# Mamba-2 scan with a silu MLP on one core: masked B^T x in PSUM, another order of weight pieces, loads and sums

## The chip, the cores and the metric

The kernel runs on one core of one Trainium2 chip. The metric is device microseconds of one execution. The engines are TensorE (PE in the profile, its weight loads PEld), VectorE (DVE), ScalarE (ACT), GpSimd (POOL) and SyncE (SP, which here only issues DMAs). Each takes its own instructions in the order in which the program lists them; between engines, semaphores hold an instruction until its inputs and buffers are ready.

## What is computed

A scan over 4 batches of 8 heads, 768 steps, head size 32 and state size 16, and an MLP on its result, 3072 tokens wide 256, with 2048 hidden units. The reference uses chunks of 32 steps; the result doesn't depend on the length of a chunk, and the kernel uses 64.

```
for c in range(nc):                      # chunks, in order
    cum = cumsum(log a)                  # within the chunk
    M = (C B^T) * exp(cum_i - cum_j) * causal
    y = M x + (C state) * exp(cum_i)
    state = exp(sum log a) * state + sum_j exp(cum_last - cum_j) B_j x_j
h = y @ w_in;  g = h / (1 + exp(-h));  out = g @ w_out
```

## The kernel before

**Units.** The work is cut into 12 units of 256 steps, three to a batch (u = 0 to 11; u % 3 == 2 is the last of its batch and needs no state after it). Each unit holds four chunks of 64 steps, t = 0 to 3, written as t = 2k + c.

**The scan of a unit** runs through these functions:
- `load_unit` issues the unit's DMAs on SP's queue: `pa` and `ab` (a in two layouts), B and C (`bn`, `tbc`), and `xt` (x). Units 1 and 2 take C in the layout of `bn`, and TensorE transposes both (`f_TP`, L333); later ones use VectorE (`f_T`, L324).
- `f_P` (L262, L268) makes prefix products of a, `f_E` (L299, L281) the decays E.
- `f_B` (L318) on POOL: BT = B times the decay to the end of the chunk. `f_C` (L349): C times the prefix.
- `f_G` is `f_D0` (L367), B^T x of each chunk by matmuls, then `f_G0` (L382), C B^T. From unit 2 on both land in one PSUM tile, `gy`, [128, 4, 512], which fills four banks and has a single buffer: C B^T in columns 0 to 255 of each bank, B^T x in columns 256 to 383 of banks 0 and 1 (the bank is c). Columns 384 to 511 are unused.
- `f_M` (L393) on VectorE multiplies C B^T into E.
- `f_D` (L402) on ScalarE: two heads share each group of 32 rows, so B^T x has blocks that mix heads. Each of four instructions copies a part with a mask (`par`) as its scale to the SBUF tile `dm`.
- `f_S` makes the states one after the other: state(t+1) = state(t) * decay + dm(t), for each chunk. The first of a batch is a copy (L416), the others one VectorE instruction (L424), except from unit 4 on for the last update of a unit, which is two POOL instructions (L421, L422).
- `f_Y` takes a new `gy` tile, in the same buffer, and writes y to it: first C times state (L444), then M x (L453). `f_X` (L462) copies it to SBUF as XM on ScalarE.

**The MLP.** `f_s1` (L473, silu L475) does h and g of a unit for 256 hidden units, j = 0 to 7; `f_s2` runs the next few matmuls of the output (L487, L564) from a list of generators. From unit 4 on, units are taken in pairs, and a 2 x 2 block product with seven products in place of eight is used: `f_x1` (L647 to L661) for h, `s2_pair` for the output. It needs sums of the operands: `f_SW` (of w_in, POOL, L619), `f_SO` (of w_out, VectorE, L518), `f_XT` (of x, POOL, L630) and `f_TS` (of g, POOL, L532). `sums(P, j)` calls `f_TS` for the parts of pair P that are due at step j.

**Weights.** They come as 8-byte floats in 16 pieces of 512 KB (0 to 7 of w_in, 8 to 15 of w_out). `w_size(n)` (ScalarE, L164, L166) and `w_bits(n)` (VectorE L174, L176, L178, then POOL L182) make float32 of piece n. There are seven raw buffers, and `w_bits(n)` ends with the DMA of piece n + 7, in SP's queue. `wu` and `wv` between the two have three buffers.

**The order** is written out by hand: what stands earlier in the program stands earlier in each engine's queue. The list `steps` interleaves `f_s1` of units 0 and 1 with weight pieces ("s5" is `w_size(5)`, "b5" `w_bits(5)`) and with unit 2's scan (letters of `scan_piece`: T transposes, E decays, B is `f_B` and `f_C`, G is `f_G`, `f_M`, `f_D` and `f_S`, Y is `f_Y` and `f_X`, S one `f_SW`). `late` does so in unit 2's loop. From there on loops run over j = 0 to 7 for unit 2 (scan of unit 3 between), for unit 3 (scans of 4 and 5 between) and for the pairs G = 2 to 5 (scan of the next pair between, `scan_plan`).

Of the kernel before, what the change touches and what calls it, by code (L numbers as in the profile page):

```python
# [8 lines left out]
FP32 = mybir.dt.float32  # L9
# [3 lines left out]
ALU = mybir.AluOpType  # L13
# [8 lines left out]
def kernel(  # L22
# [101 lines left out]
    def load_unit(u):  # L124
        load_pa(u, nc.sync)
        if 0 < u < UPB:
            load_n(u, 1, nc.sync)
        else:
            load_t(u, 0, nc.sync)
            load_t(u, 1, nc.sync)  # L130
        load_ab(u, nc.sync)
        load_n(u, 0, nc.sync)
        load_x(u, nc.sync)
# [26 lines left out]
    def w_size(n):  # L160
        if n in raw:
            u = wu[n] = wtp.tile([128, 2, WF], FP32, name="wu")
            v = wv[n] = wtp.tile([128, 2, WF], FP32, name="wv")
            nc.scalar.activation(u, raw[n][:, :, :, 1].bitcast(FP32), AF.Abs)  # L164

            nc.scalar.activation(v, raw[n][:, :, :, 0], AF.Copy, scale=2.0 ** -51, bias=2.0)  # L166

    def w_bits(n, parts=1):
        dst = w_piece(n)[1]
        if n in raw:  # L170
            u, v, hi = wu.pop(n), wv.pop(n).bitcast(U32), raw[n][:, :, :, 1]


            nc.vector.tensor_scalar(out=u, in0=u, scalar1=LEAST, scalar2=MOST, op0=ALU.max, op1=ALU.min)  # L174
            u = u.bitcast(U32)
            nc.vector.tensor_scalar(out=u, in0=u, scalar1=3, scalar2=None, op0=ALU.logical_shift_left)  # L176

            nc.vector.scalar_tensor_tensor(out=v, in0=hi, scalar=0x80000000, in1=v,  # L178
                                           op0=ALU.bitwise_and, op1=ALU.bitwise_or)
            for i in range(parts):  # L180
                fs = slice(WF // parts * i, WF // parts * (i + 1))
                nc.gpsimd.tensor_tensor(out=dst[:, :, fs].bitcast(U32), in0=u[:, :, fs], in1=v[:, :, fs], op=ALU.add)  # L182
        if n + RAW < len(W):
            load_w(n + RAW, nc.sync)
# [16 lines left out]
    load_x(1, nc.sync)  # L201
    for n in range(3, RAW):
        load_w(n, nc.sync)
    load_unit(2)


    def f_A():
# [144 lines left out]
    def f_D0(u, early=False):  # L352

        last = u % UPB == UPB - 1
        bt = BT.pop(u).rearrange("p k h n -> p k (h n)")
        xc = xt[u].rearrange("p k h d -> p k (h d)")
        n = 3 if last else 4
        if early:
            d = [ps_h.tile([128, 512], FP32, name="hp")[:, 0:128] for c in range(2)]
        else:  # L360
            DP[u] = ps_s.tile([128, 4, 512], FP32, name="gy")
            d = [DP[u][:, c, 256:384] for c in range(2)]
        d = [o.rearrange("p (k x) -> p k x", k=2) for o in d]
        for t in range(n):
            k, c = divmod(t, 2)
            for g in range(4):
                nc.tensor.matmul(out=d[c][32 * g:32 * g + 32, k],  # L367
                                 lhsT=bt[64 * c:64 * c + 64, k, 32 * g:32 * g + 32],
                                 rhs=xc[64 * c:64 * c + 64, k, 64 * g:64 * g + 64], start=True, stop=True,
                                 tile_position=(64 * c, 32 * g), skip_group_check=True)  # L370
        BX[u] = d, n

    def f_G0(u):

# [19 lines left out]

    def f_D(u, c):

        d, n = BX[u]
        if c == 0:
            DM[u] = sc.tile([128, 2, 2, 64], FP32, name="dm")
        nk = (n + 1 - c) // 2  # L400
        for e in range(2):
            nc.scalar.activation(DM[u][:, 0:nk, c, 32 * e:32 * e + 32], d[c][:, 0:nk, 32 * e:32 * e + 32],  # L402
                                 AF.Copy, scale=par[:, e:e + 1])

    def f_S(u, t0=0, t1=4):

        first, last = u % UPB == 0, u % UPB == UPB - 1
        if first and t0 == 0:
            ST[u] = sc2.tile([128, 4, 64], FP32, name="st")
        if not last and t1 == 4:  # L410
            ST[u + 1] = sc2.tile([128, 4, 64], FP32, name="st")
        for t in range(t0, min(t1, 3 if last else 4)):
            k, c = divmod(t, 2)
            o = ST[u][:, t + 1] if t < 3 else ST[u + 1][:, 0]
            if first and t == 0:
                nc.vector.tensor_copy(out=o, in_=DM[u][:, k, c])  # L416
            else:
                p = PFX[u][:, t, Q:]
                if u >= 2 * UPB - 2 and t == (2 if last else 3):

                    nc.gpsimd.tensor_tensor(out=o, in0=ST[u][:, t], in1=p.to_broadcast([128, 64]), op=ALU.mult)  # L421
                    nc.gpsimd.tensor_tensor(out=o, in0=o, in1=DM[u][:, k, c], op=ALU.add)  # L422
                else:
                    nc.vector.scalar_tensor_tensor(out=o, in0=ST[u][:, t], scalar=p,  # L424
                                                   in1=DM[u][:, k, c], op0=ALU.mult, op1=ALU.add)

    def f_GMD(u):
        f_G(u)
# [30 lines left out]
    def f_X(u):  # L459

        XM[u] = xmp.tile([128, 4, 128], FP32, name="XM")
        nc.scalar.activation(XM[u], DP.pop(u)[:, :, 0:128], AF.Copy)  # L462


    def f_s1(g, j):
        if j == 0:
            GTS[g] = gpool.tile([128, NF, UT], FP32, name="gT")
        xm = XM[g].rearrange("p (w c) t -> p w (c t)", w=2)
        hp = ps_h.tile([128, 2, UT], FP32, name="hp")
        for i in range(2):  # L470
            f = 2 * j + i
            for kc in range(KC):
                nc.tensor.matmul(out=hp[:, i], lhsT=w_in_sb[:, kc, f * 128:(f + 1) * 128],  # L473
                                 rhs=xm[:, kc], start=(kc == 0), stop=(kc == KC - 1))
        nc.scalar.activation(GTS[g][:, 2 * j:2 * j + 2], hp, AF.Silu)  # L475
        if j == 7:
            XM.pop(g)
# [295 lines left out]
    f_Ab(1, 0)  # L773
    f_Ab(1, 1)
    w_size(1)
    w_size(2)
    busy(2)
    f_Y(0)
    f_X(0)
    w_bits(1)  # L780
    f_s1(0, 0)
    f_Ek(1, 0)
    f_TP(1, True)
# [16 lines left out]
    for k in range(2):  # L800
        f_M(1, k)
    w_size(4)
    f_S(1)
    f_s1(0, 3)
    f_Y(1)
    f_X(1)
    w_bits(4)

    steps = ((1, 0, "s5"), (1, 1, "b5 s6"), (1, 2, "b6 s7"), (1, 3, "E"), (0, 4, "b7 s8"),
             (1, 4, "T B"), (0, 5, "b8 s9"), (1, 5, "G"), (0, 6, "b9 s10"), (1, 6, "b10 s11"),  # L810
             (0, 7, "Y"), (1, 7, "b11 s12"))

    def w_steps(todo):
        for step in todo.split():
# [6 lines left out]
        f_s1(g, j)  # L821
        w_steps(todo)
    load_unit(3)
    late = ("b12 s13", "b13 s14", "b14 s15 b15")
    S2.append(s2_list((0, 1)))
    for j in range(8):
        f_s1(2, j)
        scan_piece(3, j, ("", "", "T", "E", "BS", "G", "", "Y"))
        f_s2(4)
        if j < len(late):  # L830
            w_steps(late[j])
        if j in (2, 5):
            load_unit(4 + j // 3)
    def sums(P, j):

        for q in {4: (0, 1), 5: (2,), 8: (3,)}.get(j, ()):
            f_TS(P, 0, q, nc.gpsimd)
            f_TS(P, 2, q, nc.gpsimd)

    for j in range(8):  # L840
        f_s1(3, j)
        scan_piece(4, j, ("TE", "BS", "G", "Y", "", "", "", ""))
        scan_piece(5, j, ("", "", "T", "E", "BSS", "G", "Y", ""))
        scan_piece(6, j, ("",) * 7 + ("t",))
        f_s2(4)
        if j in (2, 5):
            load_unit(6 + j // 3)
        if j >= 6:
            f_SO(2 * j - 12)
            f_SO(2 * j - 11)  # L850
        if j == 7:
            for i in range(4):
                f_XT(2, i)
        if j == 5:
            sums(1, 4)
    for G in range(2, NU // 2):
        S2.append(s2_pair(G - 1))
        more = G + 1 < NU // 2
        plan = scan_plan(G + 1) if more else [([], [], []) for _ in range(8)]
        for j, (dve, act, pe) in enumerate(plan):  # L860
            waiting, PEND[:] = PEND[:], []
            f_x1(G, j, dve, act)
            for what in pe:
                what()
            for what in waiting:
                what()
            if j == 1:
                if G == 2:
                    sums(1, 5)
                sums(G - 1, 8)  # L870
            if j == 1 or j == 2:
                for q in range(4):
                    f_TS(G - 1, 2 * j - 1, q, nc.gpsimd)
            if j == 6 and more:
                for i in range(4):
                    f_XT(G + 1, i)
            sums(G, j)
            if j in (2, 5) and 2 * G + 4 + j // 3 < NU:
                load_unit(2 * G + 4 + j // 3)
    P = NU // 2 - 1  # L880
    sums(P, 8)
    S2.append(s2_pair(P, True))
    for n in range(7):
        f_s2(8)
# [37 lines left out]
```

## Time and profile before

| What | us |
|---|---|
| Median of 4 runs | 367.93 (366.99, 367.21, 368.64, 375.56) |
| Profiled execution, whole | 366.68 |
| Its span, first to last instruction | 364.8 |
| Groups (sum): L473 / L564 / L647 matmuls 128x256 | 59.6 / 56.5 / 52.8 and more |
| L424, state update on VectorE, x32 | 0.275 / 0.285 / 0.770 (least, median, most of one) |
| L421 + L422 on POOL, x8 each | 0.292 and 0.320 (medians) |
| L402, masked copy to `dm`, x40 of `gy` | 0.313 (median) |
| L532, a sum of g on POOL | 0.78 (mean) |
| L619, a sum of w_in on POOL | 2.35 |

How to read it: busy time is a sum over instructions of an engine; one of TensorE overlaps the next, so steps between starts tell its pace. A line of waits names the waiting engine and line, what ended the wait, and then the sum in us, the number of times and the longest. A timeline row has start, duration, engine, line, operation, output<-inputs, shapes and a count; in brackets stand the idle time before it and what ended it. The DMA queue issues in order, and its rows are SP's time for the issue, not the transfer. The first 29 us are start-up, in which the engines wait for loads and for one another; from there TensorE's matmuls follow one another almost without a break until 356 us.

### The profile page before, as it was taken

How to read it: one execution, taken by the hardware profiler on the slowest of the kernel's cores; microseconds unless marked ns; L12 is line 12 of the kernel's file. 1: busy time of each engine (PE TensorE's matmuls, PEld its weight loads, DVE VectorE, ACT ScalarE, POOL GpSimd, SP SyncE). 2: the span in 40 equal slices, each digit the busy share in tenths (PEclk: the TensorE clock that was granted, in tenths of full speed). 3: DMA queues.
4: the chain of work that ended last, by engine and by line, in shares of the span. 5: the costliest groups of instructions: out<-in, count | busy, mean ns of one | idle time of the engine just before them, and what ended most of it. 6: DMA issues, size and time to landing. Idle time of an engine off the chain costs nothing.

```text
span 364.8 us, 8354 instructions
## 1 busy us (share of the span) xinstructions
PE 347.7 (95%) x3277; PEld 289.5 (79%) x3279; DVE 190.4 (52%) x383; ACT 162.7 (45%) x414; POOL 188.8 (52%) x259
## 2 busy tenths in 40 slices
PE   8689899999999899999999999999999999999994
PEld 2467688788887688878887878888878888888883
DVE  7985988652348647743445742456742221213722
ACT  2565755423232444545444644544644444554100
POOL 3432344233057759896159496149595646473100
PEclk9999999999999999999999999999999999999998
DMA  6998956861545242152127034110000110001202
GB/s 141 195 273 174 353 153 113 134 114 42 109 106 72 66 78 32 17 117 38 22 52 111 14 100 52 26 16 2 14 2 6 25 16 1 14 2 17 41 2 44
DMA packets 110195, 26.53 MB, mean 73 GB/s; under 512 B 98892, under 2 KB 106060, under 8 KB 110156
## 3 DMA queue, kind: packets, MB, share of 16 engines
q1 hardware_dynamic: 107180, 25.67, 34.2%
q10 hardware_dynamic: 2976, 0.33, 0.6%
q8 instruction: 26, 0.43, 0.5%
q14 instruction: 13, 0.11, 0.1%
HBM read 22.83 MB, written 3.15 MB: 71 GB/s over the span
## 4 chain that ended last, share of the span: by engine, by line
PE 68%; POOL 9%; DVE 6%; issue 5%; DMA 5%; ACT 3%; SPq 3%; ACTq 0%; DVEq 0%; POOLq 0%
PE o_ps L564 27%; PE hp L647 24%; PE hp L473 5%; PE o_ps L487 4%; PE hp L564 3%; POOL gT L532 3%; PE gy L453 2%; POOL TN L532 2%; DMA raw<-in_moe_w_in_dram 2%; DVE wv L178 1%; PE gy L382 1%; POOL raw L619 1%; DMA xt<-in_x_dram 1%; PE gy L444 1%; ACT wu L164 1%
## 5 line engine op out<-in xcount | busy, mean ns | idle before, releaser
L650 DVE TENSOR_TENSOR gT<-hp,p 128x256 f32<-128x256 f32 x64 | 26.9, 420 | 83.1 <-ACT p L661 45.0
L473 PE MATMUL hp<-XM,w_in_sb 128*128 128x256 f32 x256 | 59.6, 381 | 4.5 <-ACT XM L462 3.3
L653 ACT ACTIVATE gT<-gT 128x256 f32<-128x256 f32 x96 | 39.8, 414 | 44.3 <-DVE gT L650 44.3
L473 PEld LDWEIGHTS hp<-XM,w_in_sb 128*128 128x128 f32 x256 | 48.0, 190 | 11.9 <-POOL w_in_sb L182 4.6
L564 PE MATMUL o_ps<-gT,w_out_sb 128*128 128x256 f32 x224 | 56.5, 379 | 0.0
L647 PE MATMUL hp<-raw 128*128 128x256 f32 x192 | 52.8, 380 | 1.5 <-POOL raw L630 1.5
L532 POOL TENSOR_TENSOR gT<-gT 128x256 f32<-128x256 f32 x72 | 54.2, 780 | 0.0
L564 PEld LDWEIGHTS o_ps<-gT,w_out_sb 128*128 128x128 f32 x224 | 42.5, 190 | 5.9
L647 PEld LDWEIGHTS hp<-raw 128*128 128x128 f32 x192 | 36.0, 190 | 7.3 <-POOL raw L630 1.9
L535 POOL TENSOR_TENSOR ps<-ps 128x256 f32<-128x256 f32 x28 | 20.3, 725 | 41.1 <-ACT ps L571 34.5
L318 POOL TENSOR_TENSOR BT<-bn,E 128x256 f32<-128x256 f32 x12 | 7.9, 654 | 60.9 <-DMA out_dram<-ot 18.4
L661 ACT ACTIVATE p<-hp 128x256 f32<-128x256 f32 x64 | 24.5, 383 | 30.2 <-PE hp L647 28.5
L475 ACT ACTIVATE gT<-hp 128x512 f32<-128x512 f32 x32 | 19.0, 598 | 39.6 <-PE hp L473 39.6
L647 PE MATMUL hp<-XM,w_in_sb 128*128 128x256 f32 x128 | 34.2, 389 | 0.0
L650 DVE TENSOR_TENSOR gT<-hp,u 128x256 f32<-128x256 f32 x32 | 13.5, 422 | 35.7 <-PE hp L647 35.7
L487 PE MATMUL o_ps<-w_out_sb,gT 128*128 128x256 f32 x128 | 31.1, 385 | 0.6 <-POOL w_out_sb L182 0.6
L532 POOL TENSOR_TENSOR TN<-gT 128x256 f32<-128x256 f32 x40 | 30.1, 772 | 0.1
L487 PEld LDWEIGHTS o_ps<-w_out_sb,gT 128*128 128x128 f32 x128 | 23.7, 190 | 4.7 <-POOL w_out_sb L182 1.0
L647 PEld LDWEIGHTS hp<-XM,w_in_sb 128*128 128x128 f32 x128 | 23.2, 189 | 4.4 <-issue 1.0
L281 DVE TENSOR_TENSOR_SCAN E<-ab,diag 128x256 f32<-128x256 f32 (+1 forms) x32 | 24.9, 819 | 2.7 <-PE gy L453 2.3
L393 DVE TENSOR_TENSOR E<-gy,E 128x512 f32<-128x512 f32 x24 | 15.4, 681 | 19.5 <-PE gy L382 15.7
L532 POOL TENSOR_TENSOR gT<-gT,TN 128x256 f32<-128x256 f32 x32 | 22.1, 728 | 0.0
(123 smaller groups left out, 556.0 us busy)
## 6 DMA issues: line engine op xcount, KB each, us to landing
ab<-in_a_dram SPq DMA_DIRECT2D x40, 128.0 KB, 3.7
raw<-in_moe_w_in_dram SPq DMA_DIRECT2D x8, 512.0 KB, 4.4
raw<-in_moe_w_out_dram SPq DMA_DIRECT2D x8, 512.0 KB, 3.6
xt<-in_x_dram SPq DMA_DIRECT2D x24, 128.0 KB, 3.4
out_dram<-ot SPq DMA_DIRECT2D x76, 32.0 KB, 1.7
pa<-in_a_dram SPq DMA_DIRECT2D x12, 128.0 KB
bn<-in_B_dram SPq DMA_DIRECT2D x22, 64.0 KB, 3.9
tbc<-in_C_dram SPq DMA_DIRECT2D x40, 32.0 KB, 1.9
```

What stands on the lines that cost most here:

```text
L281: nc.vector.tensor_tensor_scan(out=E[u].rearrange("p k h t -> p (k h t)")[:, Q * g0:Q * (g0 + n)], data0=t.rearrange("p g t -> p (g t)"), ...
L393: nc.vector.tensor_tensor(out=m[:, k], in0=DP[u][:, :, 128 * k:128 * k + 128], in1=m[:, k], op=ALU.mult)
L473: nc.tensor.matmul(out=hp[:, i], lhsT=w_in_sb[:, kc, f * 128:(f + 1) * 128], rhs=xm[:, kc], start=(kc == 0), stop=(kc == KC - 1))
L475: nc.scalar.activation(GTS[g][:, 2 * j:2 * j + 2], hp, AF.Silu)
L487: nc.tensor.matmul(out=o[:, c], lhsT=GTS[g][:, f, 128 * c:128 * c + 128], rhs=w_out_sb[:, f, :], start=(f == 0), stop=(f == NF - 1), skip_ ...
L532: engine.tensor_tensor(out=o[:, j], in0=a0[:, j], in1=a1[:, j], op=ALU.subtract)
L535: engine.tensor_tensor(out=o, in0=p, in1=q, op=ALU.add)
L564: nc.tensor.matmul(out=o, lhsT=w(j), rhs=g()[:, j], start=(j == 0), stop=(j == NF // 2 - 1))
L647: nc.tensor.matmul(out=o, lhsT=w, rhs=x_, start=start, stop=True, skip_group_check=True)
L650: nc.vector.tensor_tensor(out=o, in0=p, in1=q, op=ALU.add)
L653: nc.scalar.activation(o, i, AF.Silu)
L661: nc.scalar.activation(o, i, AF.Copy)
```

## The change

Three parts. First, for units 2 and on, ScalarE's masked copy of B^T x goes to columns 384 to 511 of the same `gy` tile, where there is room, and not to SBUF. All state updates are on VectorE and read it there; POOL's two instructions are gone. Units 0 and 1 (`early`) keep a `dm` tile in SBUF. Second, the order of the beginning: `load_unit(2)` stands behind the loads of pieces 7 and 8, `w_size(2)` behind unit 0's `f_X`, the preparation of pieces 5 to 8 stands earlier, and unit 2's E, T, B, G and Y earlier in `steps`. The last pieces get other places in `late`, and the second, third and fourth `f_SW` stand one call earlier (one of them now in unit 2's loop). Third, of the sums of g of the first pair only the first part stays in unit 3's loop, ahead of `f_XT(2, i)`; the second follows behind the first step of pair 2, and the others in its second step.

```diff
-    load_unit(2)
...
+        dm = None if early else [DP[u][:, c, 384:512].rearrange("p (k x) -> p k x", k=2) for c in range(2)]
...
-        BX[u] = d, n
+        BX[u] = d, dm, n
...
-        d, n = BX[u]
+        d, dm, n = BX[u]
         if c == 0:
-            DM[u] = sc.tile([128, 2, 2, 64], FP32, name="dm")
+            if dm is None:
+                dm = sc.tile([128, 2, 2, 64], FP32, name="dm")
+                dm = [dm[:, 0], dm[:, 1]]
+            DM[u] = dm
         nk = (n + 1 - c) // 2
         for e in range(2):
-            nc.scalar.activation(DM[u][:, 0:nk, c, 32 * e:32 * e + 32], d[c][:, 0:nk, 32 * e:32 * e + 32],
+            nc.scalar.activation(DM[u][c][:, 0:nk, 32 * e:32 * e + 32], d[c][:, 0:nk, 32 * e:32 * e + 32],
                                  AF.Copy, scale=par[:, e:e + 1])
...
             if first and t == 0:
-                nc.vector.tensor_copy(out=o, in_=DM[u][:, k, c])
+                nc.vector.tensor_copy(out=o, in_=DM[u][c][:, k])
             else:
-                p = PFX[u][:, t, Q:]
-                if u >= 2 * UPB - 2 and t == (2 if last else 3):
-
-                    nc.gpsimd.tensor_tensor(out=o, in0=ST[u][:, t], in1=p.to_broadcast([128, 64]), op=ALU.mult)
-                    nc.gpsimd.tensor_tensor(out=o, in0=o, in1=DM[u][:, k, c], op=ALU.add)
-                else:
-                    nc.vector.scalar_tensor_tensor(out=o, in0=ST[u][:, t], scalar=p,
-                                                   in1=DM[u][:, k, c], op0=ALU.mult, op1=ALU.add)
+                nc.vector.scalar_tensor_tensor(out=o, in0=ST[u][:, t], scalar=PFX[u][:, t, Q:],
+                                               in1=DM[u][c][:, k], op0=ALU.mult, op1=ALU.add)
...
     w_size(1)
-    w_size(2)
     busy(2)
     f_Y(0)
     f_X(0)
+    w_size(2)
     w_bits(1)
+    load_unit(2)
...
     w_size(4)
+    w_size(5)
     f_S(1)
     f_s1(0, 3)
     f_Y(1)
     f_X(1)
+    w_size(6)
     w_bits(4)
+    w_bits(5)
-    steps = ((1, 0, "s5"), (1, 1, "b5 s6"), (1, 2, "b6 s7"), (1, 3, "E"), (0, 4, "b7 s8"),
-             (1, 4, "T B"), (0, 5, "b8 s9"), (1, 5, "G"), (0, 6, "b9 s10"), (1, 6, "b10 s11"),
-             (0, 7, "Y"), (1, 7, "b11 s12"))
+    steps = ((1, 0, "b6 s7"), (1, 1, "E"), (1, 2, "T B b7 s8"), (1, 3, "b8 s9"), (0, 4, ""),
+             (1, 4, "G b9 s10"), (0, 5, ""), (1, 5, "Y b10 s11"), (0, 6, "b11 s12"), (1, 6, ""),
+             (0, 7, "b12 s13"), (1, 7, ""))
...
-    late = ("b12 s13", "b13 s14", "b14 s15 b15")
+    late = ("b13 s14", "b14 s15", "b15")
...
-        scan_piece(3, j, ("", "", "T", "E", "BS", "G", "", "Y"))
+        scan_piece(3, j, ("", "", "T", "E", "BS", "G", "S", "Y"))
...
-    def sums(P, j):
-
-        for q in {4: (0, 1), 5: (2,), 8: (3,)}.get(j, ()):
+    def sums(P, qs):
+
+        for q in qs:
...
-        scan_piece(5, j, ("", "", "T", "E", "BSS", "G", "Y", ""))
+        scan_piece(5, j, ("", "", "T", "E", "BS", "G", "Y", ""))
...
         if j == 5:
-            sums(1, 4)
+            sums(1, (0,))
...
+            if G == 2 and j == 0:
+                sums(1, (1,))
             if j == 1:
-                if G == 2:
-                    sums(1, 5)
-                sums(G - 1, 8)
+                sums(G - 1, (2, 3) if G == 2 else (3,))
...
-            sums(G, j)
+            sums(G, {4: (0, 1), 5: (2,)}.get(j, ()))
...
-    sums(P, 8)
+    sums(P, (3,))
```

## The prediction, made before the changed kernel had run

> **What bounds the kernel now.** First the page's table of busy times and the granted clock, to see which engine is the limit:
>
> ```profile
> PE 347.7 (95%) x3277; PEld 289.5 (79%) x3279; DVE 190.4 (52%) x383; ACT 162.7 (45%) x414; POOL 188.8 (52%) x259
> PEclk9999999999999999999999999999999999999998
> ```
>
> TensorE is busy 95% at full clock; the others have half their time free. So a change that leaves the matmuls alone can only win what TensorE stands idle, and only work that makes TensorE wait can lose. The second view is therefore the list of waits of TensorE alone (us in total, times, longest):
>
> ```profile
> PE hp L473 <- ACT XM L462: 3.3, 2, 2.5
> PE gy L444 <- POOL st L422: 1.8, 3, 0.8
> PE gy L367 <- POOL BT L318: 1.6, 1, 1.6
> PE hp L647 <- POOL raw L630: 1.5, 1, 1.5
> PE hp L473 <- POOL w_in_sb L182: 1.2, 2, 0.9
> PE o_ps L487 <- POOL w_out_sb L182: 0.6, 1, 0.6
> ```
>
> The first and fifth lie before 29.33 us (start-up); the rest lie later. Over 29.3 to 356 us the windows view gives 321.0 busy of 326.7, so at most about 6 us, and a little that modelled ends hide, is to be had there. The third view is the timeline, for where these waits stand and what stood in the queue ahead:
>
> ```profile
> 45.41 0.43 PE L367 MATMUL gy<-xt,BT 64*32 64x64 f32 x24 [1.56 <-POOL BT L318]
> ...
> 112.72 0.58 PE L444 MATMUL gy<-cw,st 32*64 32x64 f32 x24
> 113.89 0.34 PE L444 MATMUL gy<-cw,st 32*64 32x64 f32 x8 [0.59 <-POOL st L422]
> ...
> 122.74 0.70 PE L647 MATMUL hp<-raw 128*128 128x256 f32 x2 [1.48 <-POOL raw L630]
> ```
>
> The step from one start to the next is safer than a modelled end. Where nothing waits a 256-column matmul starts every 216 ns; against that the stops are 1.73 us (from 43.47), 0.75 (67.74, weight piece 15) and 1.64 (120.88, the differences of X). For the state updates I read from the first L444 to the first L453: 0.63 where nothing waits (unit 4, 32 matmuls), 0.51 with 24. Unit 5 takes 1.44, unit 6 0.72, unit 7 1.03, unit 8 1.63, unit 9 1.04, unit 10 0.63, unit 11 1.48: an excess of 0.81, 0.21, 0.40, 1.00, 0.53, 0 and 0.85, 3.8 in all. POOL's two-instruction update is behind sums in its queue there, and VectorE's own ones are slow:
>
> ```profile
> 98.12 1.01 DVE L424 SCALAR_TENSOR_TENSOR st<-st,pfx,dm 128x64 f32<-128x64 f32 x3 [0.67 <-ACT dm L402]
> ...
> 140.50 1.29 DVE L424 SCALAR_TENSOR_TENSOR st<-st,pfx,dm 128x64 f32<-128x64 f32 x2
> ```
>
> At 98 us POOL is idle and three take 1.01; at 140 us POOL runs sums and two take 1.29.
>
> **What the skill says.** "SBUF — State Buffer", Who interferes with whom: a VectorE instruction with two SBUF inputs and a GpSimd one that reads SBUF block each other wholly, while one with at most one SBUF input, outside the two-port modes, does not contend. The trace agrees: L424 runs from 0.28 to 0.77, while L650, with one PSUM input, stays at 0.42 in the middle of POOL's sums. "PSUM — Partial Sum Buffer", PSUM bank collisions: two engines must be kept from the same bank at once, reads against reads too. The trace has it as a wait: dm L402 waits on E L393 (9.4 us, 4 times), which it doesn't read. "VectorE: DVE Perf Modes", The TRN2 errata: a PSUM source costs 120 cycles fixed against 58, an estimate of 65 ns more per update; no run here shows it yet.
>
> **The change part by part.**
>
> *States from PSUM, all on VectorE (units 2 to 11).* Removed: 8 times two POOL instructions (0.29 + 0.32, 0.67 + 0.65 once). Added: 8 VectorE updates. Cost of one: between 0.22 (copy-like, below SBUF) and 0.35 (0.285 + 0.065); I take 0.29, step 0.34, because L650 with a PSUM input costs no more than its size suggests. ScalarE's write goes to PSUM instead of SBUF: 0.31 now, between 0.25 and 0.37; I take no change, as its step of 0.2 isn't what ends the wait except in odd units. Added wait: the y tile of L444 takes the same buffer as gy, so all of y waits until the last update has read dm, also the one (t = 3) that only the next unit needs. Behind that wait stands the whole TensorE queue. So, unit by unit, from the first update now:
> - Unit 5: updates end at about 112.65, y wanted at 112.72. Excess 0.81 to 0.05: 0.76.
> - Unit 6: first at 139.69, copy unblocked 0.2, three at 0.34: 140.95 against 141.40: 0.21.
> - Unit 7: ScalarE's dm ends at 161.87; the last update ends 162.85 against 162.66, so y starts 0.2 late: gain 0.2.
> - Unit 8: three from 194.41 end 195.4 against 196.12: 1.00.
> - Unit 9: end at 218.28 against 218.06: 0.53 to 0.25: 0.28.
> - Unit 10: end 251.2 against 251.56: 0. Unit 11: end 272.3 against 272.48: 0.85.
> Sum 3.3. At the dear end (0.07 more per step, up to four steps) units 5, 7 and 9 lose 0.25 each: 2.5. At the cheap end 3.7.
>
> *Sums of x before sums of g.* Before unit 3's stage ends POOL has 4 fewer sums (of 0.7 to 1.15, "113.80" to "121.97" in its timeline) ahead of the four differences at L630, and no state update. X of unit 5 is ready at 115.65, so the first difference is done by about 116.5, and TensorE wants it at 120.9. Gain 1.64. The moved four sums fall into POOL's idle 6.25 us before BT at 131.53, and the next ones stand where they stood, so nothing reads them later. The weight sums `f_SW` (2.35 each, at 73.85, 88.26 and twice from 105.92) come one call earlier: the second runs right behind the first, in an idle stretch of 10.8, and the third takes its place at 88.26. There it can hold back VectorE's prefix and clamp of unit 4, but the scan behind them waits until 84.47 anyway: 0. The 8 added updates, 2.4 us of VectorE, lie in its idle half.
>
> *Pieces 5 to 8, unit 2's scan sooner.* `w_size(2)` behind XM(0): XM starts near 13.4 instead of 15.20, the first stage 1.4 earlier. It doesn't last: the third (21.23) waits for piece 2, which is VectorE, without a break from 12.01 to 21.7, and POOL. 0. ScalarE's `w_size(5)` and `w_size(6)` (1.3 each) fall into its idle 1.31 and 2.08 before the silus at 27.12 and 31.36; were those gone, each would cost a silu at most 0.6, and three hp buffers cover that. The B-ahead-of-b7 order takes the 1.73 at 43.47 away: POOL's L182 of piece 7 (1.27) and VectorE's three for it stood ahead of BT. The last load of weights is issued earlier too, as b8 is, and unit 3's loads behind it. Piece 15 is prepared one step sooner (its ACT part ended at 66.4 for a read at 67.74; now some 3 us early): 0.75.
>
> Against that, unit 2's loads (11 issues, in SP's one queue) now stand behind pieces 7 and 8, each 512 KB. At the page's best slice, 353 GB/s, each takes 1.5 us: 3.0 later. SP's queue is full there (four ab issues take 7.28):
>
> ```profile
> 21.38 7.28 SPq L95 DMA_DIRECT2D ab<-in_a_dram  x4
> 28.71 2.23 SPq L107 DMA_DIRECT2D bn<-in_B_dram  x2
> 30.99 1.30 SPq L122 DMA_DIRECT2D xt<-in_x_dram  x2
> 32.41 0.73 SPq L156 DMA_DIRECT2D raw<-in_moe_w_in_dram  x1
> ```
>
> bn(2)'s second issue is at 29.4; with the page's 3.9 us to landing it is there at 33.3 now, at 36.4 after. The transposes of bn(2) on TensorE (L333) move from behind (1,4) at 39.6 to behind (1,2): 29.33 + 3 x 1.73 = 34.5. TensorE takes its queue in order, so all of it waits: about 2.0, between 0.8 (loads catch up) and 3.2 (landing as slow as C's 7.5 median suggests). After that nothing is late: E(2) ends near 38.3 (ab at 34.4, pieces 5 and 6 ahead of it), BT near 39, D at 42.4; state updates end near 46.5, Y(2) is wanted at 47.
>
> Sum: 3.3 + 1.64 + 1.73 + 0.75 - 2.0 = 5.4. The profiled execution took 366.68 (span 364.8 and 1.9 around it), so 361.3. The median of the runs shown is 367.93, 1.25 above it; without the one at 375.56 the middle is 367.21, 0.5 above. I add 0.6: 361.9.
>
> **The rivals.**
> - *The transposes' wait eats more, or the last update holds y more than I think* (dear ends together: 3.2, 2.5): 2.5 + 1.64 + 1.73 + 0.75 - 3.2 = 3.4, 363.9. For it: SP's queue is at its limit there. Against: packets flow without a gap, so 3.0 is firm.
> - *The loads are there in time* and the PSUM reads are cheap: 3.7 + 1.64 + 2.48 = 7.8, 359.5. For it: the listed bn landing is a median over the kernel.
> - *The updates don't decide* and y waits the same: banks keep ScalarE's second pair and VectorE's first apart until both are done, the chain M, D, S then being serial. 3.3 shrinks to 1: 364.2.
> - *Slower.* Unit 2's loads land so late that the transposes' wait carries on into D(2) and Y(2), since all queues are in order. Price: as many us as the landing of x is over 42.4, on top of the 2.0. It turns the sum negative when together they pass 7.4, x at 48 or so, 11 us over now. Then about 368.5 or more. Against it: x lands near 34.3 in the trace's packets, and 37.4 with two pieces ahead.
>
> **How the numbers follow.** The forecast 0.55, dear ends 0.17, in time 0.1, serial updates 0.1, slower 0.05, something unseen 0.03. The range 359.5 to 364.8 holds the first, and most of the next three. About 0.5% (1.8 us) can be told from no change: below 366.1 is faster. The first four cases lie there but for their far tails (0.03 of 0.92): 0.89; these tails and the unseen are the same, 0.06; slower 0.05.
>
> **What would show it.** Right: no L421/L422 group, L424 near 0.29 during POOL's sums, no wait of L444 over 0.3 after 100 us, none of L647 on raw, a wait of TensorE at L333 of about 2 us for bn's DMA near 34.5, BT(2) near 39. Wrong: L424 above 0.4, y held by DVE in each unit, no wait at L333, or a new one at L367.

## The result: slower, and the profile after

The changed kernel takes 370.84 us (median of 32 runs, 368.54 to 372.57) against 368.48 for the kernel before beside it (51 runs, 366.36 to 375.56). The ratio is 1.0077, 95% interval 1.006 to 1.0094; ratios leave out executions over 1.5% above the fastest of their kernel, so they aren't the quotients of the medians. The profiled execution took 369.51 us (span 367.8; before 366.68 and 364.8).

TensorE's work is the same, and it waits for others. From the page of after, busy us, share of the span and instructions of each engine:

```profile
PE 347.2 (94%) x3277; PEld 289.4 (79%) x3279; DVE 195.3 (53%) x391; ACT 165.2 (45%) x414; POOL 180.3 (49%) x243
```

TensorE's waits in after (us in total, times, longest):

```profile
PE hp L644 <- DVE gT L647: 4.2, 4, 3.0
PE gy L441 <- DVE st L421: 4.1, 6, 1.1
```

The waits for BT, for `raw` and for `w_out_sb` that stood here before are gone, and so is POOL as the one who holds the state up. Two new ones are larger than each of them. (Line numbers after: L441 is y's first matmul, L421 the state update, L405 the masked copy, L261 the clamp `pz` of `f_P`, L267 its scan, L529 a sum of g, L644 and L647 the MLP's matmul and the addition of its result.)

**The first loss: y waits for the updates.** Unit 4's masked copies and updates, which POOL does not disturb, in the timeline (start us, duration, engine, line). Before:

```profile
97.57 0.93 ACT L402 ACTIVATE dm<-gy,par 128x64 f32<-128x64 f32 x4 [1.95 <-DVE E L393]
...
98.12 1.01 DVE L424 SCALAR_TENSOR_TENSOR st<-st,pfx,dm 128x64 f32<-128x64 f32 x3 [0.67 <-ACT dm L402]
```

After:

```profile
97.31 1.25 ACT L405 ACTIVATE gy<-gy,par 128x64 f32<-128x64 f32 x4 [1.96 <-DVE E L393]
...
98.59 1.23 DVE L421 SCALAR_TENSOR_TENSOR st<-st,pfx,gy 128x64 f32<-128x64 f32 x4 [1.40 <-ACT gy L405]
```

Read the distance from the first copy to the first update: 0.55 us before, 1.28 after. Before, the four copies start 0.20 apart and overlap, and the first update starts after the second copy. After, each copy waits on ScalarE's own semaphore for the one ahead of it (0.32 from start to start), since all four now read and write one tile, and the first update waits for the fourth, though it reads only what the first two wrote. Then four updates follow rather than three. The updates themselves are as cheap as I had hoped: 0.281 us each (mean, none over 0.282, also beside POOL's sums), where the mean was 0.409.

The excess of y is read in TensorE's steps: by how much the first M x starts later than the undisturbed 0.63 (0.51 with 24 matmuls) behind y's first matmul, with a wait ahead of y's first matmul counted in. It is 0 in units 3 and 10 and otherwise:

| | 2 | 4 | 5 | 6 | 7 | 8 | 9 | 11 | sum |
|---|---|---|---|---|---|---|---|---|---|
| before | 0 | 0 | 0.82 | 0.21 | 0.41 | 1.01 | 0.52 | 0.87 | 3.84 |
| after | 1.15 | 0.67 | 0.30 | 0 | 0.95 | 0 | 0.89 | 0.58 | 4.54 |

**The second loss: VectorE is shut out.** The view of the tile `pz` in after (duration min/median/max, first and last start) and its timeline where the largest wait arises:

```profile
L261 DVE TENSOR_SCALAR pz<-pa x12: 265/284/5433, 8.7 to 256.8; 128x256 f32<-128x256 f32 x12
```

```profile
142.01 0.73 POOL L532 TENSOR_TENSOR ps<-ps 128x256 f32<-128x256 f32 x1
...
142.58 0.42 DVE L647 TENSOR_TENSOR gT<-hp,p 128x256 f32<-128x256 f32 x1 [1.74 <-ACT p L658]
142.69 5.51 POOL L529 TENSOR_TENSOR gT<-gT 128x256 f32<-128x256 f32 x8
142.92 5.43 DVE L261 TENSOR_SCALAR pz<-pa 128x256 f32<-128x256 f32 x1
...
148.39 0.70 DVE L267 TENSOR_TENSOR_SCAN pfx<-pz,one 128x260 f32<-128x260 f32 x1
```

A clamp of 0.28 us takes 5.43: it starts inside the first of eight sums on POOL and ends when the eighth has ended. It happens in each of the three pairs (2.96 at 201.15, 2.93 at 256.77). VectorE takes its queue in order, so the L647 behind it frees no PSUM buffer, and TensorE's step grows by 3.18 us at 146.06, 0.71 at 204.29 and 0.67 at 259.91. The first of these stops:

```profile
149.46 0.70 PE L644 MATMUL hp<-raw,w_in_sb 128*128 128x256 f32 x2 [3.02 <-DVE gT L647]
```

The same place before:

```profile
144.41 0.29 POOL L421 TENSOR_TENSOR st<-st,pfx 128x64 f32<-128x64 f32 x1
144.50 0.42 DVE L650 TENSOR_TENSOR gT<-hp,p 128x256 f32<-128x256 f32 x1 [1.32 <-ACT p L661]
144.78 0.32 POOL L422 TENSOR_TENSOR st<-st,dm 128x64 f32<-128x64 f32 x1
144.84 0.41 DVE L262 TENSOR_SCALAR pz<-pa 128x256 f32<-128x256 f32 x1
...
145.06 4.09 POOL L532 TENSOR_TENSOR gT<-gT 128x256 f32<-128x256 f32 x5
...
145.28 1.10 DVE L268 TENSOR_TENSOR_SCAN pfx<-pz,one 128x260 f32<-128x260 f32 x1
```

Here POOL's two state instructions stand ahead of the sums. The second reads what the first wrote, so that POOL is idle for 0.08 us between them, and the clamp gets in at once.

**The sum.** From the start of the first `f_s1(1, 0)` to the last matmul after takes 1.9 us more (331.87 against 329.98): BT -1.73, piece 15 -0.75, X of unit 5 -1.64, y +0.70, the clamps +4.56, two steps of 0.33 and 0.14 behind the last pair +0.47: together +1.6, with 0.3 left in smaller steps. The other 1.05 of the span's 3.0 lie in the start-up, where the page has a dip in TensorE's granted clock (40 slices, in tenths of full speed; the second digit):

```profile
PEclk9899999999999999999999999999999999999999
```

From 7.6 to 11.0 us it is half, and unit 0's y starts at 13.51, against 12.02 before. The new order isn't the cause: of the kernels below, the first part alone, which begins as before, has the same dip from 7.9 on and starts y at 13.41, and those that begin as the changed kernel does have no dip there and start it at 11.86 to 12.43. The wait of the transposes is absent in this execution; in the kernels below with the new beginning it is 0.7 to 2.2 us.

### The profile page after: what moved, and what is told of

Its sections match the earlier page's. It is cut to its first block, busy times and chain, and to the rows that moved or that the text cites. A ratio compares the mean times of both kernels' runs of the same rounds, so it can differ in the third digit from the quotient of the medians.

```text
span 367.8 us, 8347 instructions
## 1 busy us (share of the span) xinstructions
PE 347.2 (94%) x3277; PEld 289.4 (79%) x3279; DVE 195.3 (53%) x391; ACT 165.2 (45%) x414; POOL 180.3 (49%) x243
## 4 chain that ended last, share of the span: by engine, by line
PE 81%; DVE 10%; ACT 4%; DMA 2%; issue 2%; POOL 0%; SPq 0%; ACTq 0%; DVEq 0%
PE o_ps L561 26%; PE hp L644 25%; PE hp L470 12%; PE o_ps L484 7%; DVE pz L261 3%; PE hp L561 3%; PE gy L450 2%; PE gy L382 2%; PE gy L441 2%; ACT gy L405 2%; DVE st L421 2%; DVE wv L178 1%; DVE E L393 1%; PE gy L367 1%; DVE pfx L267 1%
## 5 line engine op out<-in xcount | busy, mean ns | idle before, releaser
L647 DVE TENSOR_TENSOR gT<-hp,p 128x256 f32<-128x256 f32 x64 | 26.8, 419 | 78.9 <-ACT p L658 44.7
L644 PE MATMUL hp<-raw 128*128 128x256 f32 x192 | 52.7, 380 | 0.2 <-DVE gT L647 0.2
L529 POOL TENSOR_TENSOR gT<-gT 128x256 f32<-128x256 f32 x72 | 50.7, 734 | 0.0
L644 PEld LDWEIGHTS hp<-raw 128*128 128x128 f32 x192 | 36.2, 190 | 5.8 <-POOL ps L532 0.9
L644 PE MATMUL hp<-XM,w_in_sb 128*128 128x256 f32 x128 | 34.1, 389 | 0.0
L647 DVE TENSOR_TENSOR gT<-hp,u 128x256 f32<-128x256 f32 x32 | 13.6, 424 | 36.5 <-PE hp L644 36.5
L529 POOL TENSOR_TENSOR TN<-gT 128x256 f32<-128x256 f32 x40 | 29.3, 748 | 2.2 <-ACT gT L650 2.2
L644 PEld LDWEIGHTS hp<-XM,w_in_sb 128*128 128x128 f32 x128 | 23.3, 190 | 4.3 <-issue 1.0
L644 PE MATMUL hp<-raw,w_in_sb 128*128 128x256 f32 x64 | 19.5, 386 | 4.1 <-DVE gT L647 4.1
```

Of the source, the lines that this page charges most:

```text
L529: engine.tensor_tensor(out=o[:, j], in0=a0[:, j], in1=a1[:, j], op=ALU.subtract)
L644: nc.tensor.matmul(out=o, lhsT=w, rhs=x_, start=start, stop=True, skip_group_check=True)
L647: nc.vector.tensor_tensor(out=o, in0=p, in1=q, op=ALU.add)
```

## The experiments

"Excess of y" and "TensorE's step" are read as above, and ratios are to the kernel before, run beside each on the same chip. There it went from 366.4 to 376 us, with its median at 367.8 to 368.6.

### Which part loses

**The second and third part alone**: the updates as before.

```diff
-        dm = None if early else [DP[u][:, c, 384:512].rearrange("p (k x) -> p k x", k=2) for c in range(2)]
+        dm = None
...
+                p = PFX[u][:, t, Q:]
+                if u >= 2 * UPB - 2 and t == (2 if last else 3):
+                    nc.gpsimd.tensor_tensor(out=o, in0=ST[u][:, t], in1=p.to_broadcast([128, 64]), op=ALU.mult)
+                    nc.gpsimd.tensor_tensor(out=o, in0=o, in1=DM[u][c][:, k], op=ALU.add)
+                else:
...
```

> The changed kernel with its first part undone: the masked copy goes to SBUF and POOL does the last update again; order of pieces, loads and sums as changed. If the first part alone loses (theory A: every update waits for all four masked copies, and POOL's sums run without a break and shut VectorE out), the three stops of 1.73, 0.75 and 1.64 us are gone and nothing comes in their place: 362 to 364, a ratio of 0.985 to 0.992 to the kernel before; L441 waits as before (about 2 us on POOL's L42x) and VectorE's pz (L261) under 1 us. If the new order loses (theory B: later loads of unit 2, sums of g at another place), the time stays near 369 to 371.

Measured: 363.72 us (20 runs), ratio 0.9926 (0.9895 to 0.9956). Thirteen runs lie at 363.1 to 364.4, seven at 365.7 to 368.1; the profiled one is of the latter (367.69). In it another instruction is shut out, unit 6's copy of its first state:

```profile
134.65 5.50 POOL L535 TENSOR_TENSOR gT<-gT,TN 128x256 f32<-128x256 f32 x8
...
136.10 4.79 DVE L419 COPY st<-dm 128x64 f32<-128x64 f32 x1
```

Unit 6's y has an excess of 3.61 us by it, near the distance between the two groups. So the order is a gain, and being shut out, which I hadn't expected here, is not tied to `pz`.

**The first part alone**: the kernel before with its updates from PSUM, the change's own lines on `dm` and the update and no others.

```diff
+        dm = None if early else [DP[u][:, c, 384:512].rearrange("p (k x) -> p k x", k=2) for c in range(2)]
...
-                if u >= 2 * UPB - 2 and t == (2 if last else 3):
...
```

> The kernel before with the first part of the change alone: masked copy in PSUM, all updates on VectorE. Theory A: slower, 369 to 373, with a wait of TensorE for VectorE's L647-like sums near 146 us of 2 to 3 us, and waits of y's first matmuls in units 2, 4, 5, 7, 9, 11. Theory B: the first part gains some 1 to 3 us, 364 to 366.

Measured: 371.14 us, ratio 1.0096 (1.0073 to 1.0119). The clamps take 5.44, 2.95 and 2.91 us, the excess of y in units 4 to 11 is 0.67, 0.30, 0, 0.95, 0, 0.89, 0 and 0.59, together 3.40. So both losses come from the first part.

**The third part alone** and **the second part alone** on the kernel before, each with the change's own lines. Of the third:

```diff
-            sums(1, 4)
+            sums(1, (0,))
...
+            if G == 2 and j == 0:
+                sums(1, (1,))
...
```

Of the second:

```diff
-    load_unit(2)
...
+    w_size(2)
     w_bits(1)
+    load_unit(2)
...
-    steps = ((1, 0, "s5"), (1, 1, "b5 s6"), (1, 2, "b6 s7"), (1, 3, "E"), (0, 4, "b7 s8"),
+    steps = ((1, 0, "b6 s7"), (1, 1, "E"), (1, 2, "T B b7 s8"), (1, 3, "b8 s9"), (0, 4, ""),
...
```

> The kernel before with the third part of the change alone (sums of x ahead of sums of g). The stop of 1.64 us at the differences of X goes, nothing else moves: 1.2 to 2 us faster, 365 to 366.5 against 366.7 to 367.9. If later sums of g hold back anything, no gain or a loss.

> The kernel before with the second part of the change alone (pieces 5 to 8, unit 2's loads and its scan sooner; the updates as before, the sums of g ahead). My theory: the stop at BT (1.73 us) and piece 15's (0.75 us) go, some 1.3 us come back as a wait of the transposes for bn: 0.5 to 2.0 us faster, 365.5 to 367. If the sooner order itself is what lets VectorE run into GpSimd's unbroken sums, a stall of 3 to 5 us shows at 136 or 142 us and the time is 369 to 372.

Measured: the sums alone 366.47 us, ratio 0.9965 (0.9937 to 0.9993); the stop for unit 5's X is gone, y as before. The front alone 365.68 us, ratio 0.992 (0.9883 to 0.9956); the stops at BT and at piece 15 are gone, TensorE's steps at the four transposes are 2.12 longer together, 1.62 of it in the first, for bn's DMA. Nothing was shut out in either profiled execution.

**All updates on VectorE, but from SBUF**: one line of the changed kernel.

```diff
-        dm = None if early else [DP[u][:, c, 384:512].rearrange("p (k x) -> p k x", k=2) for c in range(2)]
+        dm = None
```

> The changed kernel with the masked copy in SBUF, all updates still on VectorE. If it is the place in PSUM that makes copies follow each other at 0.32 and the first update wait for all four, copies go back to 0.20 and the first update starts after two; y's waits in units 2, 4, 5 fall from 1.24, 0.75, 0.39 to under 0.2 each. But updates have two SBUF inputs again, so in units 6 to 11 they wait for POOL's sums (0.6 to 0.8 each, or shut out for a whole run of sums). Since pz is shut out as in the changed kernel, time 367 to 371. If placement doesn't matter, y's waits stay as they are.

Measured: median 370.66 us (20 runs), as expected, but in two groups: six at 361.7 to 363.0 us, the others at 369.9 to 384.6. The profiled one took 371.0: up to there the excess of y in units 2, 4 and 5 is 0 (the copies overlap again: it is the placement in the tile that they read that makes the first loss), and at 190.41 one update is shut out for 7.88 us:

```profile
190.41 8.59 DVE L421 SCALAR_TENSOR_TENSOR st<-st,pfx,dm 128x64 f32<-128x64 f32 x3
```

Unit 8's y has an excess of 6.7 us by it. TensorE's granted clock then is at half for 10 us (194.7 to 204.9), in the page's row of 40 slices:

```profile
PEclk9999999999999999999995999999999999999999
```

None of the six at 361.7 to 363.0 was profiled. That nothing is shut out in them is inferred from the two groups: it looks like a lottery, with one draw where VectorE first needs the ports that it shares with POOL in each run of sums.

### What lets VectorE in

**Two dependent small additions** where POOL's update stood, on a tile of their own:

```diff
+        if u >= 2 * UPB - 2 and t1 == 4:
+            for _ in range(2):
+                nc.gpsimd.tensor_tensor(out=nop, in0=nop, in1=nop, op=ALU.add)
```

> The changed kernel with two small POOL instructions, the second dependent on the first, where the last update stood (units 4 to 11). Theory A1 (the first VectorE instruction that needs the port pair in an unbroken run of POOL's sums isn't let in before the run's end): the pair stands just ahead of the second run of sums in the first pair of units, about when pz comes, so the 5.43 there may fall under 1 us, while pz at 201 and 257 comes in the middle of the run, long after the pair, and still takes 2.5 to 3 us; time down by 0 to 3 us, 367.5 to 370.5. If any dependent pair in the run is enough, all three fall: 365 to 367. If pz waits for something else, nothing moves.

Measured: 363.98 us (363.61 to 364.21), ratio 0.9904 (0.9868 to 0.9939). Work was added and 6.9 us of the median went, more than any of the cases expected. The excess of y is that of after from unit 4 on; the clamps are let in:

```profile
142.12 0.59 POOL L427 TENSOR_TENSOR nop<-nop 128x16 f32<-128x16 f32 x2
142.67 2.49 POOL L534 TENSOR_TENSOR gT<-gT 128x256 f32<-128x256 f32 x3
...
142.35 0.28 DVE L263 TENSOR_SCALAR pz<-pa 128x256 f32<-128x256 f32 x1
```

In the other two pairs the clamp comes 2.4 us behind the additions, in the midst of the sums, and takes 0.66 and 0.65: it waits for one sum, not for the run, as the second case had it and not the first.

**A dependent small addition after every two sums**, in the changed kernel and in the one with the updates as before:

```diff
+        if engine is nc.gpsimd and i in (1, 3):
+            nc.gpsimd.tensor_tensor(out=nop, in0=o[:, j, 0:16], in1=o[:, j, 0:16], op=ALU.add)
```

> The changed kernel with one small POOL instruction behind every two sums of the two long runs, which reads the sum just written, so that the run has a break each 1.4 us. Theory A1: pz takes under 1.7 us in every pair, TensorE's stops of 3.18, 0.71 and 0.67 us at 146, 204 and 260 go, y's waits stay (units 2, 4, 5, 7, 9, 11: some 4 us): time 364.5 to 367, a ratio to the kernel before of 0.99 to 1.0. If the port isn't the cause, pz stays at 3 to 5 us and the time near 370 to 371.

> The changed order with the masked copy in SBUF and the last update on POOL, as in the run of the order only, plus the breaks. That run had times near 363.4 and, in 5 of 20, near 367.9, with a state copy of 4.79 us in the profiled one of the latter. Theory A1: the second group of times goes, and all lie between 362.5 and 365. Against it: one in four still near 368. The difference to the changed kernel with breaks is what the place in PSUM and the updates on VectorE cost without the shutting out: 1.5 to 3 us by y's waits if theory A holds, under 0.5 if the shutting out was all.

Measured: 365.25 us, ratio 0.9936 (0.991 to 0.9962), and 366.18, ratio 0.9964 (0.9943 to 0.9985). Neither has an instruction shut out in its profiled execution. The first came as expected. The second did not: its two groups became one, but at 364.9 to 367.5 and not at 362.5 to 365. There POOL's update stands behind a longer run, and unit 8's y has an excess of 2.18 (1.01 before); what else the additions cost wasn't taken apart, so this pair doesn't price the place in PSUM.

**One addition ahead of the second run**, first free, then reading the last sum of the run before. The free one:

```diff
+            if j == 2:
+                nc.gpsimd.tensor_tensor(out=nop[:, 0:16], in0=nop[:, 16:32], in1=nop[:, 16:32], op=ALU.add)
             if j == 1 or j == 2:
                 for q in range(4):
                     f_TS(G - 1, 2 * j - 1, q, nc.gpsimd)
```

> The changed kernel with one more small GpSimd add (128x16, on a tile of its own, waiting for nothing) just ahead of the second run of eight sums in each pair of units. The pair of dependent adds that let VectorE in stood at this place. Theory 1: any extra instruction that breaks the rhythm of the sums is enough: VectorE's pz (5.43, 2.96 and 2.93 us in the changed kernel) takes under 1 us in all three places, and the time is 364 to 365.5. Theory 2: what counts is on what the sums of the second run wait; an instruction that waits for nothing leaves that as it is, pz stays shut out for 3 to 5 us, and the time is 369 to 372.

The reading one, at the same place:

```diff
-                nc.gpsimd.tensor_tensor(out=nop[:, 0:16], in0=nop[:, 16:32], in1=nop[:, 16:32], op=ALU.add)
+                b11 = gb(G - 1, 0, 0)[:, 7, 0:16]
+                nc.gpsimd.tensor_tensor(out=nop[:, 0:16], in0=b11, in1=b11, op=ALU.add)
```

> The same small GpSimd add at the same place, but it reads the last sum of the run before, so that it takes the wait on GpSimd's own earlier result once for all. Theory 1 (any instruction is enough) and theory 2 (the wait of the sums on GpSimd's own results counts) both expect pz under 1 us and 363.5 to 365.5; if theory 2 alone holds, this one is faster than its sister by 5 us or more, and if neither holds both stay at 369 to 372.

Measured: 369.76 us, ratio 1.0052 (1.0029 to 1.0074), and 370.52, ratio 1.0055 (1.0031 to 1.008). Both theories fell: the clamps take 5.66 and 5.62 us, in the other pairs about 3. The reading one waits for a sum that had ended one instruction earlier, so POOL doesn't stop for it:

```profile
140.84 0.73 POOL L534 TENSOR_TENSOR ps<-ps 128x256 f32<-128x256 f32 x1
141.52 0.22 POOL L877 TENSOR_TENSOR nop<-gT 128x16 f32<-128x16 f32 x1
141.70 5.51 POOL L531 TENSOR_TENSOR gT<-gT 128x256 f32<-128x256 f32 x8
```

Each starts before its predecessor has ended: 140.84 + 0.73 is past 141.52, and 141.52 + 0.22 past 141.70. In the trace the sums behind it no longer wait on POOL's own semaphore, as they do with the free one, so that wait isn't what shuts VectorE out. That gave the third theory, on pauses, and its tests.

**The two small additions without the dependence**:

```diff
-            for _ in range(2):
-                nc.gpsimd.tensor_tensor(out=nop, in0=nop, in1=nop, op=ALU.add)
+            for i in range(2):
+                nc.gpsimd.tensor_tensor(out=nop[:, 16 * i:16 * i + 16], in0=diag[:, 0, 0:16], in1=diag[:, 0, 0:16], op=ALU.add)
```

> The changed kernel with two small GpSimd adds at the place where the two dependent ones stood, but independent of each other: each reads a constant and writes columns of its own. Theory 3 (VectorE gets in where GpSimd has paused, even for 0.08 us, not long before; in all traces so far VectorE's first instruction for the pair was shut out in 12 of 12 cases where GpSimd had run 12.6 us or more without a pause, in 2 of some 14 at 7.8 to 8.2 us, and in none within 3.8 us of one): the second add starts before the first has ended, no pause arises, pz is shut out again for 3 to 5 us, and the time is 369 to 372. Theory 4 (two instructions more on GpSimd at that place are what helps): pz takes under 1 us, 363.5 to 364.5, as with the dependent ones.

And **the dependent two ahead of the first run of sums**, in place of the updates:

```diff
+            if j == 1:
+                for _ in range(2):
+                    nc.gpsimd.tensor_tensor(out=nop, in0=nop, in1=nop, op=ALU.add)
             if j == 1 or j == 2:
                 for q in range(4):
                     f_TS(G - 1, 2 * j - 1, q, nc.gpsimd)
```

> The changed kernel with the two dependent small adds ahead of the first run of eight sums rather than of the second, so that GpSimd pauses some 6 us before pz rather than 0.3 to 2.4 us before it. If a pause anywhere within the last 7 us is enough mostly: pz under 1 us in most of the three places and 363.5 to 366. If the pause must lie between the two runs: pz shut out in all three, 369 to 372.

Measured, without the dependence: 370.89 us, ratio 1.0075 (1.0048 to 1.0103), all clamps shut out.

```profile
141.52 0.39 POOL L427 TENSOR_TENSOR nop<-diag 128x16 f32<-128x16 f32 x2
141.87 5.51 POOL L534 TENSOR_TENSOR gT<-gT 128x256 f32<-128x256 f32 x8
...
141.75 5.78 DVE L263 TENSOR_SCALAR pz<-pa 128x256 f32<-128x256 f32 x1
```

Two instructions at the same place: 0.59 us with the dependence, 0.39 without (they read a constant and not their own tile). The dependence, and with it the pause, is what differs, and it is worth 6.9 us of the median. Of the 6.6 between the two profiled executions, 5.6 are TensorE's steps at the three clamps. Another 1.8 come from its granted clock, half for 3.4 us from 148.9, just behind the longest stop, and 1.0 goes the other way at the transposes. Such a stretch of 3.4 to 10.2 us at half clock lies in or behind the longest stop in five of the seven profiled executions that have one of over 3 us past the start-up, not in that of the changed kernel.

With the pause ahead of the first run, 6.1 to 8.6 us before the clamps: 365.34 us, ratio 0.9922 (0.9898 to 0.9945), from 363.5 to 368.6; in the profiled one (363.67) all three got in. The first:

```profile
142.00 0.46 DVE L263 TENSOR_SCALAR pz<-pa 128x256 f32<-128x256 f32 x1
```

The table takes the 16 profiled executions and asks, for each stretch of POOL's instructions without a pause, what happened to VectorE's first instruction without a PSUM operand in it (memsets left out, and transposes, which take 0.64 us in the midst of POOL's sums as without them), where at least three of POOL's were still to start:

| Since POOL's last pause | Shut out to the end of the run |
|---|---|
| up to 3.8 us | 0 of 38 |
| 6.1 us | 0 of 1 |
| 7.8 to 8.6 us | 2 of 18 |
| 12.6 to 13.1 us | 15 of 15 |

All 15 in the last row are clamps, at the same three places of five kernels; with a pause 6.1 to 8.6 us before it the same clamp got in, three times of three. Time since the pause and the number of POOL's instructions since then aren't told apart.

Where VectorE had got in once, its later instructions in the same run waited for one POOL instruction at most: in the execution with the updates from SBUF the copy got in at 135.65, and the clamp at 140.79 took 0.46, though POOL went on without a pause.

### A version without either loss

**The two dependent additions, and the four copies put into two**, each over both banks, in the units with four chunks:

```diff
+        if u >= 2 and n == 4:
+            if c == 0:
+                w = DP[u][:, 0:2, 256:512].rearrange("p c (i k x) -> p i c k x", i=2, k=2)
+                for e in range(2):
+                    nc.scalar.activation(w[:, 1, :, :, 32 * e:32 * e + 32], w[:, 0, :, :, 32 * e:32 * e + 32],
+                                         AF.Copy, scale=par[:, e:e + 1])
+            return
```

> The changed kernel with the two dependent GpSimd adds, and with the four masked copies of a unit put into two (each takes both banks at once) in the units that have four chunks (3, 4, 6, 7, 9 and 10). If y is late in these units because four copies of 0.29 us run one after another in one tile, y's excess wait falls in units 4, 7 and 9 from 0.67, 0.95 and 0.89 us to under 0.45 each, stays in units 5, 8 and 11, and the time is 362 to 363. If a copy of twice the elements costs twice as much, nothing is gained: 363.5 to 364.5.

And the same with the pause only ahead of the second run of each pair (four places, the last with no clamp behind it):

```diff
-        if u >= 2 * UPB - 2 and t1 == 4:
-            for _ in range(2):
-                nc.gpsimd.tensor_tensor(out=nop, in0=nop, in1=nop, op=ALU.add)
...
+            if j == 2:
+                for _ in range(2):
+                    nc.gpsimd.tensor_tensor(out=nop, in0=nop, in1=nop, op=ALU.add)
```

> The merged copies with the two dependent adds moved from the updates of each unit to one place for each pair of units, just ahead of the second run of eight sums (three places rather than eight). Theory 3: the pause before the second run is the only one that is needed; pz stays under 1 us and the time is as with all eight, 361.5 to 362.5. If the other five pauses let other work in too, one of those instructions is shut out and the time is 363 to 366.

Measured: 362.04 us (361.89 to 362.82), ratio 0.983 (0.9766 to 0.9894), and 362.18 (361.53 to 362.54), ratio 0.9839 (0.9797 to 0.9882). A copy of 128 elements takes 0.340 us, one of 64 0.287. The excess of y in units 4, 7 and 9 fell to 0.13, 0.42 and 0.35, and stayed in 5 and 11, as expected. Unit 4 in the last one:

```profile
97.05 0.72 ACT L409 ACTIVATE gy<-gy,par 128x128 f32<-128x128 f32 x2 [1.96 <-DVE E L395]
...
97.80 1.23 DVE L430 SCALAR_TENSOR_TENSOR st<-st,pfx,gy 128x64 f32<-128x64 f32 x4 [0.87 <-ACT gy L409]
```

From the first copy to the first update it is 0.75, after 1.28. In its list of TensorE's waits nothing like the wait for L647 is left, and the pauses at the one place do what all did. Behind the wait of the start-up for `w_in_sb` the list goes on with:

```profile
PE gy L450 <- DVE st L430: 1.3, 4, 0.5
PE o_ps L217 <- DVE gT L212: 1.3, 1, 1.3
PE gy L334 <- DMA bn<-in_B_dram: 1.3, 2, 1.0
```

## Why the prediction was wrong

It said 361.9 us, faster; the kernel is at 370.84, slower. Step by step:

- *"The 8 added updates ... lie in its idle half" and "Removed: 8 times two POOL instructions"*: the step that turned the sign. The removal was costed at nothing or a gain. These instructions held the only pause in POOL's runs near the clamps, and the profile before shows it: POOL's second one at 144.78, and the clamp at 144.84. The kernels without a pause there lose 4.6 to 5.6 us of TensorE's steps at the clamps; with the pause put back, and nothing else, the median falls by 6.9. (The change took away VectorE's earlier uses of the ports by updates from SBUF, too; with those kept and no pause, six of 20 executions took 363 us or less.) No rival named it; my "slower" one put the loss on unit 2's loads, which don't cause it (the front alone is faster).
- *"ScalarE's write goes to PSUM ... I take no change, as its step of 0.2 isn't what ends the wait"*: wrong in kind. A copy is no dearer in itself (0.287 against 0.316 for 64 elements), but its program waits: four in a row in one tile, and the update behind all four. The 3.3 us for the states shrank to 0.44 (3.84 to 3.40, the first part alone). The rival of serial updates, 1 us, came nearest, but not for its reason: in unit 4 the first update, which reads bank 0, waited for the copies in bank 1 as well, and merging the copies in the same banks won back 1.6 of the 2.5 us in units 4, 7 and 9. The gains of units 6 and 8 came in full, those of 5 and 11 in part, and 4, 7 and 9 lost.
- *Cost of an update, 0.29*: right, 0.281, also beside sums. "SBUF — State Buffer", Who interferes with whom, says that a VectorE instruction with at most one SBUF input, outside the two-port modes, doesn't contend with GpSimd: so it is here. The extra cost of a PSUM source, for which I had taken 65 ns as the dear end from "VectorE: DVE Perf Modes", The TRN2 errata, did not show: 0.281 against a median of 0.285 from SBUF.
- *Sums of x, 1.64; BT, 1.73; piece 15, 0.75*: right, each stop is gone in the changed kernel and in the part alone. The first part by itself also takes the stop for X away, presumably because POOL's update no longer stands ahead.
- *Transposes, -2.0*: the mechanism right, the size too, with the front alone (2.12). Elsewhere with the same beginning it goes from 0.7 to 2.2 (1.69 with the dependent additions, 1.11 with the second and third part), and it is 0 in the profiled execution of after, which starts late; that this is why isn't shown.

With both losses mended the kernel takes 362.0 to 362.2 us. That this is the number forecast is partly luck: the states then bring less than 3.3 (1.8 in the last one), and the transposes cost less than 2.0 (1.66).

## What to carry to other kernels

Ask of an instruction that is taken away not only who waits for it, but what its own waits let others do: a pause of 0.08 us in POOL's queue was worth some 5 us to TensorE, two engines further. Where VectorE and POOL need the same ports, don't let POOL run for long without a pause ahead of a VectorE instruction that TensorE waits for; the first losses here came at 7.8 us. Two dependent tiny instructions were enough here, independent ones were not. And when an intermediate moves into the tile that it is computed from, count the semaphores: writes that overlapped before may follow one another.

## What the hardware showed unexpectedly

"SBUF — State Buffer", Who interferes with whom, says that the engine that issues first has the shared ports for its whole instruction, and that the other is blocked until then. Mostly VectorE waits for no more than that here (0.66 us for a clamp of 0.28), but after a long run of POOL without a pause it lost to some four to twelve instructions in a row: 5.43 us in the changed kernel, 7.88 at most, always until the run ended. Why a pause, or having got in once, prevents it, no run shows; the table gives only how it goes with the time since the pause, and the step from 8.6 to 12.6 us wasn't tried. Part of the spread of the kernel before may come from the same draw, as its first state update of a pair comes 7.8 to 8.2 us after a pause; its one profiled run took 366.68, so that stays open.
